# One attention and feed-forward kernel: where the output weights' sums are made, which banks the queries behind a burst use, and which queue carries loads and stores

## The chip, the cores and the metric

The kernel runs on one core of a Trainium2 chip, from one launch. Its time is the device time in microseconds of that core. The kernel before was run 11 times: median 587.55 us, lowest 582.9, highest 592.51. One further execution was recorded by the hardware profiler and took 585.29 us; the recorded span, from its first to its last instruction, is 583.5 us. Every time of day in this text ("at 247.48") is counted in microseconds from the start of that span.

## The reference

All inputs are bfloat16. There are 2048 tokens with 448 features, 16 query heads on 8 key/value heads of width 256, and a feed-forward width of 1792. Attention looks at the last 512 keys of the cache, without a mask.

```python
xn = layernorm(x)                                  # no weights, eps 1e-5
q  = xn @ wq                                       # [2048, 448] @ [448, 16*256]
k, v = k_cache[:, :, -512:], v_cache[:, :, -512:]  # each serves two query heads
p  = softmax(q @ k.T * 256**-0.5)
s  = (p @ v) @ wo                                  # [2048, 16*256] @ [4096, 448]
g  = silu((gelu(xn @ w_gate) * (xn @ w_up)) @ w_down)
out = x + s * g
```

## The kernel before

**Engines and order.** Each engine runs its instructions in the order in which the program emits them. The class `Plan` records every operation with the buffers that it reads and writes, and from these it works out the semaphore waits; nothing is reordered, and there is no cost model. `K.reuse` gives a buffer the readers and writers of whatever held the same memory before it, so that the first write waits for them. DMAs are issued from SP's, ScalarE's (ACT) and Pool's instruction streams. A DMA whose data or whose buffer is not ready holds up everything behind it in the same stream. VectorE is DVE in the code.

**Feed-forward phase (0 to about 115 us).** The layer norm makes xn, tile by tile of 128 tokens. Pool computes the reciprocal standard deviation (`ln_rstd_pool`), VectorE normalises (`ln_norm`), and DMA transposes the tile. The loop over `n` handles two units in a pass, a unit being one block of 128 of the 1792 columns for one chunk of 512 tokens; there are 56 units. TensorE makes gate and up, ScalarE takes gelu (`gu_evac`), VectorE multiplies. Down projections (`down`) stand between passes, for chunks 0 and 1 in this phase and for chunks 2 and 3 beside the first two heads of attention. Their results, the gate values g2, go to memory by SP's queue and are loaded again a tile at a time (`load_g2`, Pool's queue; the profile calls the tile `g` and the memory `g_all`).

In the pass `n == 32` the loads for attention are emitted: Wq and V on Pool's queue, K on SP's queue as DMA transposes, then the output weights wo (`load_wt`) and three tiles of the residual x (`xr`) on Pool's queue.

**Attention.** `m` counts 64 pairs of chunk and head. Queries are made in groups: before the heads `m` = 0, 4, 12, 18, 26, 34, 42, 50 and 58, `q_group` makes two heads at a time, on the four banks of PSUM named AB or the four named BB, in turn. `s_mm(m)` makes the scores of a head in four pieces on AB. ScalarE takes the exponential with its row sum, VectorE the reciprocal and the normalised `pn`, SP issues a DMA transpose of `pn` for every two pieces. `pv(m - 2)` multiplies with V on BB two heads later. The query banks are copied to qT by ScalarE (first bank of a head) and VectorE (second bank).

**Output product.** For chunks 0 to 2 it is a fast product of 2 by 2 blocks with seven block products. `burst(c)` runs it behind the heads 17, 33 and 49. It needs seven operands `wt[:, j]` that are blocks of wo, times 64, and their sums and differences in float16, and sums of the attention outputs (`sr`). The operands are made by `make_wt` on VectorE, three instructions per head in heads 2 to 13, from `wtb`, which lies in the same memory. The 448 output columns are split as 384 + 64; the 384 into two blocks of 192. In the layout before, a block is 128 consecutive columns and 64 further ones, so each block is loaded in two pieces, with rows of 256 and 128 bytes; the second piece waits for the first, as both write the same buffers. The seven products of a burst use B1, B5, B3 and B7, which are the banks BB, and B6 and BN, which are the first two of AB. VectorE and ScalarE add them up (`part`, `fold`) and SP transposes the sums in three DMAs to `sT`. All writes to the source of these transposes wait for the transpose before (one set of buffers, `bx`).

The four tiles of the chunk are finished in the following four heads, by `burst_end` after `pv`; I call them the finishing steps. `wo_end` multiplies with g2, adds the residual in `xr` and stores the tile by SP's queue; `load_next` then loads on Pool's queue the residual of three tiles later into the same slot, which waits for the store, and behind it g2 of two tiles later.

The last chunk is multiplied directly with wo (`wo_mm`, `wo_fin`). Its four loads, on Pool's queue, go into the memory of `wt`, each as soon as the operands below it have been read by the last burst.

Of the kernel before, what the change touches and what calls it, by code (L numbers as in the profile page):

```python
# [5 lines left out]
ACT = mybir.ActivationFunctionType  # L6
ALU = mybir.AluOpType
# [161 lines left out]
def bass_recurrent_scan__sliding_block_cached__geglu_ffn__prompt_kernel(  # L169
# [41 lines left out]
    with es:  # L211
# [62 lines left out]
        NB = 4  # L274
        wt, a_wt, a_w3 = place("wt", [P, 7, Hq, N2], F16)
        wtb, _, _ = place("wtb", [P, 7, Hq, N2], BF16, at=rw)
        b_wt = [[K.buf(rw + (j * Hq + i * Hq // NB) * N2 * 2, Hq // NB * N2 * 2) for i in range(NB)] for j in range(7)]
        w3, _, rw_end = place("w3", [P, NCO, R], F16)
        w3b, _, _ = place("w3b", [P, NCO, R], BF16, at=a_w3)
        b_w3 = [K.buf(a_w3 + i * NCO // NB * R * 2, NCO // NB * R * 2) for i in range(NB)]  # L280
# [68 lines left out]
        def dma(q, o, i, reads=(), writes=()):  # L349
            K.op(q, lambda e, o=o, i=i: e.dma_start(o, i), reads, writes, dma=True)  # L350
# [4 lines left out]
        def act(o, i, func, reads, writes, scale=1.0):  # L355
            K.op("act", lambda e, o=o, i=i: e.activation(o, i, func, scale=scale), reads, writes)  # L356

        def add(eng, o, x, y, reads, writes, op=ALU.add):
            K.op(eng, lambda e: e.tensor_tensor(o, x, y, op), reads, writes)  # L359
# [248 lines left out]
            dma_t(kT[:, g, :, :], A_k_cache[0, g, Sk - W:Sk, :], (), (b_kT[g],))  # L608

        def load_v(g):  # L610
            dma("pool", va[:, g, :, :],
                A_v_cache[0, g, Sk - W:Sk, :].rearrange("(j p) d -> p j d", p=P), (), (b_va[g],))

        def load_wq(g):
            lo, hi = g * HG * Dh, (g + 1) * HG * Dh
            dma("pool", wq[:, :, lo:hi], A_wq[0:K3, lo:hi].rearrange("(k p) f -> p k f", p=P), (), (b_wql[g][0],))
            for e in range(2):
                dma("pool", wqr[R * e:R * e + R, g * HG:(g + 1) * HG, :],
                    A_wq[K3:D, lo:hi].rearrange("p (h e f) -> p h e f", e=2, f=P)[:, :, e, :], (), (b_wql[g][1 + e],))

        wo_view = A_wo.rearrange("(h e p) d -> p e h d", e=2, p=P)
        M1, M2 = slice(0, P), slice(P, N2)

        def load_wt():
            K.reuse([b for x in b_wt for b in x] + b_w3)
            for j, e, n in ((0, 0, 0), (4, 0, 1), (2, 1, 1), (1, 1, 0)):
                dma("pool", wtb[:, j, :, M1], wo_view[:, e, :, n * P:n * P + P], (), b_wt[j])
                dma("pool", wtb[:, j, :, M2], wo_view[:, e, :, 2 * P + n * R:2 * P + n * R + R], (), b_wt[j])
            dma("pool", w3b[:, :, :], A_wo.rearrange("(c p) d -> p c d", p=P)[:, :, D - R:D], (), b_w3)

        def make_wt():
            for i in range(NB):
                hs = slice(i * Hq // NB, (i + 1) * Hq // NB)
                cs = slice(i * NCO // NB, (i + 1) * NCO // NB)
                for o, x, b in [(wt[:, j, hs, :], wtb[:, j, hs, :], b_wt[j][i:i + 1]) for j in (0, 4, 2, 1)] + [
                        (w3[:, cs, :], w3b[:, cs, :], b_w3[i:i + 1])]:
                    yield K.op("dve", lambda e, o=o, x=x: e.tensor_scalar(o, x, WS, None, op0=ALU.mult), b, b)
                for o, x, y in ((6, 2, 4), (4, 4, 0), (5, 2, 4), (3, 1, 5)):
                    yield add("dve", wt[:, o, hs, :], wt[:, x, hs, :], wt[:, y, hs, :],
                              [b_wt[x][i], b_wt[y][i]], b_wt[o][i:i + 1], ALU.subtract)  # L640

        DOWN_AT = {NF + 5: 0, 2 * NF + 1: 1}
        gu_evac(0, 0)
# [5 lines left out]
        for n in range(4, NU, 2):  # L649
            gu_group((n, n + 1), cur)  # L650
            gu_evac(n, cur[0])
            ln_b()
            gu_evac(n + 1, cur[1])
            if ln_t[0] < 8 or n >= 12:
                ln_a()
            cur, nxt = nxt, cur
            if n == 4:
                load_x("sp", 12, 4)
            if n == 8:
                dma("sp", wd[:, :, :], B_w_down.rearrange("(f p) d -> p f d", p=P), (), (b_wd,))  # L660
            if n == 32:
                for g in range(NG):
                    load_wq(g)
                for g in range(Hkv):
                    load_v(g)
                for g in range(Hkv):
                    load_k(g)
                load_wt()
                for t in range(NXR):
                    dma("pool", xr[:, t, :], x_view[:, t, :], (), b_xr[t])  # L670
            if n + 1 in DOWN_AT:
                down(DOWN_AT[n + 1], cur)
                cur, nxt = nxt, cur
# [59 lines left out]
        def wo_end(t, c0, c1, src):  # L733

            s, x, g = t % 2, t % NXR, t % NG2
            hv = [i for i in range(2) if (c0 < CUT, c1 > CUT)[i]]
            bt = [b_tmp[s][i] for i in hv]
            bx = [b_xr[x][i] for i in hv]
            for lo, hi, i, f, reads in src:
                K.op("dve", lambda e, lo=lo, hi=hi, i=i, f=f: e.scalar_tensor_tensor(  # L740
                    out=tmp[:, s, lo:hi], in0=i, scalar=f, in1=g2[:, g, lo:hi],
                    op0=ALU.mult, op1=ALU.mult), list(reads) + [b_g2[g]], bt)
            add("dve", xr[:, x, c0:c1], tmp[:, s, c0:c1], xr[:, x, c0:c1], bt + bx, bx)
            dma("sp", out_view[:, t, c0:c1], xr[:, x, c0:c1], bx, ())

        def load_next(t):
            if t + NXR < NT:
                dma("pool", xr[:, t % NXR, :], x_view[:, t + NXR, :], (), b_xr[t % NXR])
            if t + NG2 < NT:
                load_g2(t + NG2)  # L750

        def load_g2(t):
            dma("pool", g2[:, t % NG2, :], g2d[t], (b_g2d[t],), (b_g2[t % NG2],))

        def wo_fin(c, t4, b, c0=0, c1=D):
            t = c * 4 + t4
            wo_end(t, c0, c1, [(c0, c1, bank[b][:, c0:c1], 0.5, (b_ps[b],))])
            if c1 == D:
                load_next(t)

        o_view = oTh.rearrange("p (h e) (r q) -> p e r h q", e=2, r=2)
        HALF = (slice(0, R), slice(R, P))
# [1 line left out]
        def product(j, b, rhs, hs, first, reads):  # L764

            lst = []

            def pair(lo, hi, l0, r0, l1, r1, st):
                for u, l, r in ((0, l0, r0), (1, l1, r1)):
                    lst.append((bank[b][HALF[u], lo:hi], l, r, st, False))  # L770
            for h in hs:
                pair(0, HC, wt[:, j, h, 0:R], rhs(h), wt[:, j, h, R:P], rhs(h), first and h == hs[0])
            for h in hs[::2]:
                pair(HC, QC, wt[:, j, h, M2], rhs(h), wt[:, j, h + 1, M2], rhs(h + 1), False)
            mms(lst, reads + [b_wt[j][i] for i in sorted({h * NB // Hq for h in hs})], (b_ps[b],))

        def burst(c):
# [70 lines left out]
        def burst_end(c, t4):  # L848
            t = c * 4 + t4
            u = t4 // 2  # L850
            f = 0.5 / (WS * WS)
            wo_end(t, 0, D, [(0, D - R, sT[:, t4, :, :].rearrange("p k n -> p (k n)"), f, b_sT),
                             (D - R, D, sN[:, t4 % 2, u * R:u * R + R], f, (b_sN,))])
            load_next(t)

        LAG = 2
        late = []
# [6 lines left out]
        for m in range(NS):  # L864
            if m in groups:
                for i in range(m, groups[groups.index(m) + 1], 2):
                    q_group(i, (cur, nxt)[i // 2 % 2])
                if m == 0:
                    K.reuse([b for x in b_pT for b in x] + b_pn + b_p32)
            if m > Hq and m % Hq == LAG:  # L870
                K.reuse(b_pn + b_p32)
            s_mm(m)
            if LAG <= m < Hq:
                for x in range(3):
                    next(todo, None)
            if m < LAG:
                down(NQC - LAG + m, nxt)
                if m == LAG - 1:
                    K.reuse(b_oT + [b for y in b_qT[:QS - Q0] for b in y])
                    todo = make_wt()  # L880
                    K.reuse(b_sT + [b_sN])
                    for t in range(NG2):
                        load_g2(t)
            if len(late) == LAG:
                pv(late.pop(0))
            if m > Hq and LAG <= m % Hq < LAG + 4:
                burst_end(m // Hq - 1, m % Hq - LAG)
            if m > Hq and m % Hq == LAG - 1:
                burst(m // Hq - 1)
                if m // Hq == NQC - 1:  # L890
                    K.reuse(b_wo)
                    for i in range(NCO // 8):
                        dma("pool", wo[:, i * 8:(i + 1) * 8, :],
                            A_wo.rearrange("(c p) d -> p c d", p=P)[:, i * 8:(i + 1) * 8, :], (), (b_wo[i],))
            late.append(m)
# [72 lines left out]
```

## Time and profile before

| What | us |
|---|---|
| median of 11 runs | 587.55 |
| profiled execution | 585.29 |
| its span | 583.5 |
| TensorE busy in the span | 554.7 |
| VectorE busy | 376.5 |
| ScalarE busy | 285.8 |
| Pool busy | 52.8 |
| TensorE waits for ScalarE's exponentials | 12.2 |
| TensorE waits for VectorE behind a burst | 8.2 |
| VectorE waits for g2 | 13.3 |

PE is TensorE's multiplication, PEld its loading of weights, DVE is VectorE, ACT ScalarE, POOL Pool; SPq, ACTq and POOLq are the issues of DMAs. A row of the timeline has start, length, engine, line, operation, `out<-in`, and in brackets the idle time before it with what ended it. In a table by stretch, the busy time of each engine (with its instructions) is followed by the granted TensorE clock (1.00 is full speed), the share of time in which the 16 DMA engines were busy, and GB/s. A share can exceed 1, since packets overlap. Waits are inferred: a wait for several things is put down to the one that came last.

### The profile page before, as it was taken

To read this page: it belongs to the slowest core of one execution; us is meant where nothing else is said; L and a number is where in the kernel's file an instruction comes from. 1 tells how busy PE (TensorE), PEld (TensorE's weight loads), DVE (VectorE), ACT (ScalarE), POOL (GpSimd) and SP (SyncE) were. 2 spreads that over 40 slices of the span, in tenths; PEclk is the share of its full clock that TensorE was granted. 3 is DMA by queue.
4 is the path that set the end of the run, shared out by engine and by line. 5 is a ranking of instruction groups with operands and counts; after the bars stand their busy time and mean duration, and the time that the engine had idled before them with its cause. 6 is when DMAs were issued, how large, how long until landed. Compare 5 with 4: busy or idle time off the path is not lost.

```text
span 583.5 us, 11613 instructions
## 1 busy us (share of the span) xinstructions
PE 554.7 (95%) x4444; PEld 288.4 (49%) x4444; DVE 376.5 (65%) x952; ACT 285.8 (49%) x751; POOL 52.8 (9%) x89
## 2 busy tenths in 40 slices
PE   9999999999999899989699998997999989899998
PEld 5554444445443347934244487443445953334455
DVE  6674534443789789549657883687479637876812
ACT  5433333443577485137557830576487115666700
POOL 1120621330000000000200000020000110200001
PEclk9999999999999999999899999998999989989999
DMA  9631599862335557016953830089167362982711
GB/s 290 129 113 42 155 322 157 149 165 76 80 74 127 91 95 124 7 28 114 165 107 72 152 73 19 10 170 174 41 127 156 88 198 44 175 166 49 154 23 56
DMA packets 173479, 66.46 MB, mean 114 GB/s; under 512 B 157872, under 2 KB 169136, under 8 KB 173424
## 3 DMA queue, kind: packets, MB, share of 16 engines
q1 hardware_dynamic: 167552, 48.37, 41.3%
q0 software_dynamic: 5104, 16.78, 11.3%
q8 instruction: 35, 0.57, 0.4%
q10 hardware_dynamic: 768, 0.57, 0.3%
q14 instruction: 20, 0.16, 0.1%
HBM read 23.43 MB, written 3.67 MB: 46 GB/s over the span
## 4 chain that ended last, share of the span: by engine, by line
PE 73%; DVE 14%; DMA 8%; issue 4%; ACT 1%; POOL 0%; DVEq 0%; ACTq 0%
PE bank L365 72%; DVE pn L703 5%; DMA pT<-pn 3%; DMA sT<-xnT 2%; DMA g<-g_all 2%; DVE rden L702 2%; DVE oTh L723 1%; DVE tmp L740 1%; DVE tmp L359 1%; PE bank L482 1%; ACT p L699 1%; DVE xnT L359 1%; DVE wt L359 1%; DVE xr L359 0%; DVE cc L359 0%
## 5 line engine op out<-in xcount | busy, mean ns | idle before, releaser
L699 ACT ACTIVATE p<-bank 128x512 f32<-128x512 f32 x256 | 150.0, 599 | 52.3 <-DVE pn L703 33.8
L703 DVE TENSOR_SCALAR pn<-p,rden 128x512 bf16<-128x512 f32 x256 | 124.6, 487 | 14.7 <-DMA pT<-pn 5.7
L365 PE MATMUL bank<-kT,qT 128*128 128x512 bf16 x512 | 123.1, 381 | 11.2 <-ACT p L699 10.9
L365 PE MATMUL bank<-pT,va 128*128 128x512 bf16 x512 | 125.1, 389 | 2.9 <-DMA pT<-pn 2.6
L365 PE MATMUL bank<-xnT,wq 64*128 64x512 bf16 x768 | 96.5, 380 | 10.7 <-DVE cc L359 8.2
L365 PEld LDWEIGHTS bank<-kT,qT 128*128 128x128 bf16 x512 | 48.8, 98 | 76.5 <-ACT p L699 15.6
L365 PEld LDWEIGHTS bank<-pT,va 128*128 128x128 bf16 x512 | 50.2, 100 | 68.7 <-DMA pT<-pn 8.3
L365 PE MATMUL bank<-xnT,wgu 64*128 64x512 bf16 (+2 forms) x768 | 84.0, 350 | 0.1
L356 ACT ACTIVATE qT<-bank 128x512 bf16<-128x512 f32 x64 | 38.2, 597 | 64.1 <-PE bank L365 62.5
L686 DVE CAST qT<-bank 128x512 bf16<-128x512 f32 x64 | 42.5, 689 | 40.1 <-PE bank L365 40.1
L365 PEld LDWEIGHTS bank<-xnT,wq 64*128 64x128 bf16 x768 | 36.7, 95 | 59.2 <-DVE cc L359 9.0
L531 DVE TENSOR_TENSOR actT<-bank,gl 128x512 bf16<-128x512 f32 x56 | 37.8, 689 | 33.3 <-PE bank L365 26.6
L356 ACT ACTIVATE gl<-bank 128x512 bf16<-128x512 f32 x56 | 33.2, 597 | 49.4 <-PE bank L365 46.2
L365 PEld LDWEIGHTS bank<-xnT,wgu 64*128 64x128 bf16 x768 | 37.1, 94 | 37.0 <-issue 0.7
L699 ACT ACTIVATION_READ_ACCUMULATOR p<-bank 128x1 f32 x256 | 52.9, 207 | 0.0
L702 DVE RECIPROCAL rden<-rsum 128x1 f32<-128x1 f32 x256 | 40.1, 157 | 14.2 <-ACT p L699 14.0
L365 PE MATMUL bank<-wd,actT 128*128 128x448 bf16 x224 | 43.1, 353 | 0.0
L350 POOL DMA_DIRECT2D xr<-in_A_x_dram x16 | 9.0, 564 | 359.8 <-DVE rden L702 204.8
L723 DVE TENSOR_SCALAR oTh<-bank 128x512 f16<-128x512 f32 x48 | 32.8, 684 | 0.1
L365 PEld LDWEIGHTS bank<-wd,actT 128*128 128x128 bf16 x224 | 21.8, 98 | 21.0 <-issue 0.4
L365 PE MATMUL bank<-sr,wt 128*64 128x256 f16 x576 | 31.9, 273 | 0.0
L365 PEld LDWEIGHTS bank<-sr,wt 128*64 128x64 f16 x576 | 31.5, 110 | 0.0
(64 smaller groups left out, 420.8 us busy)
## 6 DMA issues: line engine op xcount, KB each, us to landing
wo<-in_A_wo_dram POOLq DMA_DIRECT2D x4, 896.0 KB, 6.6
wq<-in_A_wq_dram POOLq DMA_DIRECT2D x2, 1536.0 KB, 9.4
va<-in_A_v_cache_dram POOLq DMA_DIRECT2D x8, 256.0 KB, 12.9
wtb<-in_A_wo_dram POOLq DMA_DIRECT2D x4, 512.0 KB, 9.6
pT<-pn SPq DMA_TRANSPOSE x128, 2.8
g_all<-g2w SPq DMA_DIRECT2D x16, 112.0 KB, 1.7
xr<-in_A_x_dram POOLq DMA_DIRECT2D x16, 112.0 KB, 3.4
g<-g_all POOLq DMA_DIRECT2D x16, 112.0 KB, 4.4
```

What stands on the lines that cost most here:

```text
L350: K.op(q, lambda e, o=o, i=i: e.dma_start(o, i), reads, writes, dma=True)
L356: K.op("act", lambda e, o=o, i=i: e.activation(o, i, func, scale=scale), reads, writes)
L359: K.op(eng, lambda e: e.tensor_tensor(o, x, y, op), reads, writes)
L365: ins = e.matmul(o, lhsT=l, rhs=r, start=st, stop=sp, skip_group_check=True)
L482: ins = e.matmul(bank[b][:, 0:w], lhsT=gl[:, 0, 0:P], rhs=gl[:, 0, 0:w], start=True, stop=True)
L531: K.op("dve", lambda e: e.tensor_tensor(actT[:, c % 2, f, :], bank[b + 1], gl[:, s, :], ALU.mult), (b_ps[b + 1], b_gl[s]), (b_actT[c % 2][ ...
L686: K.op("dve", lambda v, s=s, b=b: v.tensor_copy(qT[:, s, 1, :], bank[b + 1]), (b_ps[b + 1],), (b_qT[s][1],))
L699: K.op("act", lambda e, b=b, r=r, z=z: e.activation(p32[:, z, :], bank[b], ACT.Exp, scale=att_scale, accum_out=rsum[:, r:r + 1]), (b_ps[b] ...
L702: K.op("dve", lambda e, r=r: e.reciprocal(rden[:, r:r + 1], rsum[:, r:r + 1]), (b_rsum[r],), (b_rden[r],))
L703: K.op("dve", lambda e, r=r, z=z, y=y, t=t4 % 2: e.tensor_scalar(pn[:, y, t, :], p32[:, z, :], rden[:, r:r + 1], None, op0=ALU.mult), (b_p ...
L723: K.op("dve", lambda v, i=i, b=b, o=o, f=f: v.tensor_scalar(o[:, i, :], bank[b], f, None, op0=ALU.mult), (b_ps[b],), (b_oT[i],))
L740: K.op("dve", lambda e, lo=lo, hi=hi, i=i, f=f: e.scalar_tensor_tensor(out=tmp[:, s, lo:hi], in0=i, scalar=f, in1=g2[:, g, lo:hi], op0=ALU ...
```

## The change

It has five pieces.

- The operands `wt` take other places in the same memory, given by `WAT`: operand 0 lies in place 6, 1 in 3, 2 in 4, 3 in 2, 4 in 5, 5 in 1, 6 in 0. Operands 0 and 4 and the last 64 columns (`w3`) lie outside the memory of x and xn.
- A block of wo is now 192 consecutive columns, loaded in one DMA with rows of 384 bytes. Blocks for operands 0 and 4 and w3 are emitted in the pass `n == 14`, those for 2 and 1 in the pass `n == 30`. The casts with the factor 64 are done by ScalarE (`cast_wt`) from pass 18 on, the subtractions by VectorE (`sum_wt`) from pass 32 on, one in a pass, and from 40 and 44 on two. Operand 6 is computed as 5 minus 0. `make_wt` and its calls in heads 2 to 13 are gone.
- Wq and V are loaded by SP's queue, ahead of K.
- `q_group` begins each set of queries with AB, except for the set before head 12, which begins with BB. Before, the sets at heads 18, 26, 34, 42, 50 and 58 began with BB and that at 12 with AB.
- In `wo_end`, the load of g2 is emitted before the store, the store of all tiles but the last four goes to Pool's queue, and the residual load follows it. A finishing step multiplies with g2 in three instructions instead of two (256, 128 and 64 elements instead of 384 and 64), because of the new order of columns.

```diff
+        WAT = [6, 3, 4, 2, 5, 1, 0]
+        b_wt = [[K.buf(rw + (j * Hq + i * Hq // NB) * N2 * 2, Hq // NB * N2 * 2) for i in range(NB)] for j in WAT]
...
         def load_v(g):
-            dma("pool", va[:, g, :, :],
+            dma("sp", va[:, g, :, :],
...
-            dma("pool", wq[:, :, lo:hi], A_wq[0:K3, lo:hi].rearrange("(k p) f -> p k f", p=P), (), (b_wql[g][0],))
+            dma("sp", wq[:, :, lo:hi], A_wq[0:K3, lo:hi].rearrange("(k p) f -> p k f", p=P), (), (b_wql[g][0],))
...
+        def load_wt(j, e, n):
+            dma("pool", wtb[:, WAT[j], :, :], wo_view[:, e, :, n * N2:(n + 1) * N2], (), b_wt[j])
+
+        def cast_wt(j, i):
...
+            act(o[:, sl, :], x[:, sl, :], ACT.Copy, b[i:i + 1], b[i:i + 1], scale=WS)
+
+        def sum_wt(o, x, y, i):
+            hs = slice(i * Hq // NB, (i + 1) * Hq // NB)
+            add("dve", wt[:, WAT[o], hs, :], wt[:, WAT[x], hs, :], wt[:, WAT[y], hs, :],
+                [b_wt[x][i], b_wt[y][i]], b_wt[o][i:i + 1], ALU.subtract)
+
+        CASTS = [(18, (j, i)) for j in (0, 4, 7) for i in range(NB)] + [(40, (j, i)) for j in (2, 1) for i in range(NB)]
+        SUMS = [(32, (4, 4, 0, i)) for i in range(NB)] + [
+            (44, (o, x, y, i)) for i in range(NB) for o, x, y in ((5, 2, 4), (6, 5, 0), (3, 1, 5))]
...
+            if n == 14:
+                load_wt(0, 0, 0)
+                load_wt(4, 0, 1)
+                dma("pool", w3b[:, :, :], A_wo.rearrange("(c p) d -> p c d", p=P)[:, :, D - R:D], (), b_w3)
+            if n == 30:
+                K.reuse([b for j in (1, 2, 3, 5, 6) for b in b_wt[j]])
+                load_wt(2, 1, 1)
+                load_wt(1, 1, 0)
+            for i in range(2 if n >= 40 else 1):
+                if CASTS and n >= CASTS[0][0]:
+                    cast_wt(*CASTS.pop(0)[1])
+            for i in range(2 if n >= 44 else 1):
+                if SUMS and n >= SUMS[0][0]:
+                    sum_wt(*SUMS.pop(0)[1])
...
-            dma("sp", out_view[:, t, c0:c1], xr[:, x, c0:c1], bx, ())
-
-        def load_next(t):
-            if t + NXR < NT:
-                dma("pool", xr[:, t % NXR, :], x_view[:, t + NXR, :], (), b_xr[t % NXR])
-            if t + NG2 < NT:
+            if t + NG2 < NT and c1 == D:
                 load_g2(t + NG2)
+            dma("sp" if t >= NT - 4 else "pool", out_view[:, t, c0:c1], xr[:, x, c0:c1], bx, ())
+            if t + NXR < NT and c1 == D:
+                dma("pool", xr[:, x, :], x_view[:, t + NXR, :], (), b_xr[x])
...
-            wo_end(t, 0, D, [(0, D - R, sT[:, t4, :, :].rearrange("p k n -> p (k n)"), f, b_sT),
-                             (D - R, D, sN[:, t4 % 2, u * R:u * R + R], f, (b_sN,))])
-            load_next(t)
+            two = lambda x, lo, hi: x[:, 0:2 * N2].rearrange("p (n d) -> p n d", n=2)[:, :, lo:hi]
+            wo_end(t, 0, D, [(lambda x: two(x, 0, P), sT[:, t4, 0:2, :], f, b_sT[:2]),
+                             (lambda x: two(x, P, N2), sT[:, t4, 2, :].rearrange("p (n d) -> p n d", n=2), f, b_sT[2:]),
+                             (lambda x: x[:, 2 * N2:D], sN[:, t4 % 2, u * R:u * R + R], f, (b_sN,))])
...
-                    q_group(i, (cur, nxt)[i // 2 % 2])
+                    q_group(i, (cur, nxt)[((i - m) // 2 + (m == Q0 + QS)) % 2])
...
-            if LAG <= m < Hq:
-                for x in range(3):
-                    next(todo, None)
```

## The prediction

> **What bounds the kernel now.** I read the page first. TensorE is busy for 554.7 of 583.5 us, so 28.8 us is all that a better order can return, unless a stall also slows the clock. Then the table of waits, to see what TensorE waited for, and who waited for the rest:
>
> ```profile
> PE 554.7 (95%) x4444; PEld 288.4 (49%) x4444; DVE 376.5 (65%) x952; ACT 285.8 (49%) x751; POOL 52.8 (9%) x89
> ...
> PE bank L365 <- ACT p L699: 12.2, 7, 4.0
> DVE tmp L740 <- DMA g<-g_all: 13.3, 4, 5.0
> PE bank L365 <- DVE cc L359: 8.2, 3, 2.7
> ```
>
> The columns of a wait are total us, times, longest. Busy time by stretch puts them in place (stretch, length, PE, PEld, DVE, ACT, POOL, granted clock, DMA share, GB/s):
>
> ```profile
> 110.00:148.00 38.00, 38.00 (x239) 18.43 (x236) 16.49 (x39) 17.71 (x43) 7.99 (x9) 1.00 0.46 116
> 170.00:196.00 26.00, 23.37 (x110) 9.67 (x107) 24.93 (x78) 18.09 (x57) 0.00 (x0) 1.00 0.65 119
> 243.00:252.00 9.00, 6.27 (x102) 5.06 (x98) 4.25 (x9) 1.24 (x3) 0.00 (x0) 1.00 0.14 29
> 280.00:300.00 20.00, 15.63 (x73) 6.16 (x72) 13.30 (x40) 10.53 (x32) 2.14 (x4) 0.91 0.85 153
> 467.00:484.00 17.00, 13.09 (x146) 7.73 (x144) 7.10 (x16) 3.63 (x7) 1.76 (x2) 0.90 0.53 166
> ```
>
> The feed-forward phase has no gap. The gaps are where VectorE makes the weights' sums (170 to 196, VectorE 24.93 of 26), right behind each burst (243, 360, 471), and in the four finishing steps behind a burst (280 to 300, and their like at 394 and 509). The timeline shows that last stall whole:
>
> ```profile
> 278.17 0.54 POOL L350 DMA_DIRECT2D xr<-in_A_x_dram  x1 [6.45 <-DVE rden L702]
> 278.70 0.62 POOL L350 DMA_DIRECT2D g<-g_all  x1
> ...
> 283.97 0.56 DVE L740 SCALAR_TENSOR_TENSOR tmp<-sT,g 128x384 f32<-128x384 bf16 x1 [3.58 <-DMA g<-g_all]
> ...
> 286.69 1.03 PE L365 MATMUL bank<-kT,qT 128*128 128x512 bf16 x2 [4.04 <-ACT p L699]
> 287.51 3.20 PE L365 MATMUL bank<-pT,va 128*128 128x512 bf16 x8
> ```
>
> Pool's queue holds the residual load xr until the SP store of the same slot has landed, the gate load g2 stands behind it, VectorE waits 3.58 us for g2, the exponentials wait for VectorE, TensorE waits 4.04 us and then runs at half clock: its eight matmuls take 3.20 us where others take 1.89.
>
> **Part 1, sums of the weights.** VectorE loses 16 casts of 353 ns, 4 of 287 and 16 subtractions of 555 (15.7 us) in heads 2 to 13. There its starts of a head's first normalisation lie 4.18 us apart (165.59 to 194.86 over 7 heads), against 3.45 us of TensorE (two blocks of eight in 1.73 each). Without them VectorE needs about 3.0. The stalls they cause are 1.00, 0.15, 0.28 and, for the query group of head 12, 1.32: **-2.75 us**. In the feed-forward phase the same work is hidden: a pass of two units is 3.02 us of a full TensorE; ScalarE has 1.25 us in it and gets one or two casts of 768 elements, 0.81 us each (from its 597 ns for 512 and 381 for 256), at most 2.87; VectorE has 1.34 and gets at most two subtractions, 2.45. Uncovered they would cost 15.4 and 8.9 us. The first cast waits in ScalarE's order for its data, and ahead of VectorE's work for tile 10 Pool has three more issues (1.15 + 1.15 + 1.68 = 4.0 us from 35.8, so that a normalisation at 38.9 waits 1.8 us). Both delays fall into the ten microseconds of the first down projection (40 to 51), which needs neither: 0.
>
> **Part 2, loads moved.** Wq and V (14 issues, some 0.6 us each by SP's row for w_down) go from Pool's queue to SP's, ahead of the K transposes and behind the gate stores that end at 76.5. 5.5 MB at the 350 GB/s seen at 76 to 84 is 16 us, so the first K lands near 100; its scores start at 120.8. The weight loads lose the second piece and the wait between pieces (13.6 us at most) and go to 36 to 50 and 65 to 78, where DMA is at 0.15 to 0.5. They are needed at 52 and 94: 0.
>
> **Part 3, score banks first.** The burst's products end at 247.48; the first query group now starts at 250.21, on banks that VectorE frees last. On the score banks it starts at 247.5; the second starts at 250.5, when those banks are free (250.15). The third, at 253.5, needs VectorE's copies of the first, which stand behind the four folds, which wait for the transpose sT: the first copy ends at 254.55, as before. So 1.1 of 2.73 us comes back one group later; the third group starts at 254.6 for 256.25: **-1.65 us, twice**. The later groups, and heads 26, 42 and 58, I put at 0 (their score banks are emptied while the value product runs; at the other end a 0.25 us gap goes or comes).
>
> **The third burst is different.** There sT needs 7.07 us, not 2.4, beside the loads of wo, so VectorE's copies start at 482.7 and the third group at 483.4, whatever the order of the banks. The new places of the weights in memory delay wo: its first quarter overlaps operands that are read to 467 (issued at 458.8 now), the other three the one read last, 471.6. So three loads instead of two leave from 471.9 on. The two hold the DMA engines to 480.3 and sT lands at 481.0. One more is 0.92 MB at about 320 GB/s, 2.9 us: third group at 486.3 for 483.4. TensorE then has stood from 477.6 on and comes back at half clock; the same drop cost 1.53 us at 474 (16 matmuls in 3.26 for 1.73), but there behind the wait. Together **+4.4 us**. Here the Trainium skill speaks for less: *DMA: Bandwidth & Descriptors*, Queues, rings and completion order, has an engine take turns between queues packet by packet. By that sT would need at most twice 2.4 us whatever stands in the other queue, the third load would add nothing, and the sum would be 1.5. The row, where it landed only 0.7 us after the loads ended, decides for 4.4; 1.5 stays as the low end, 6 as the high one (sT of the step before is slowed too).
>
> **Part 4, order of Pool's queue.** The g2 load now stands ahead of store and residual load. Counted from the first finishing step of a burst: store issued at 1.5, landed by 6.5 (SP's take 1.7 us; for a store on Pool, which no row shows, I take 5, near the 5.6 of its slowest residual load; the low end is 1.7), residual load issued to 7.0, then the critical g2, landed 5.3 later at 12.3. Its reader comes at 13.2. So VectorE's waits of 3.58, 3.01 and 1.70 go. The half-clock stretches behind them go too: 0.42 + 1.31, 1.32 + 0.41, and 1.59. On this *TensorE: Matmul & The Clock Gate*, Why this matters for your kernels, warns of gaps over some 3 us; here gaps of 4.04 and 3.29 dropped the clock, and so did one of 2.13, while two of 2.73 did not. By the page the third stretch would have to be left in (1.6 us less gained); the row takes it out. Against it, each finishing step has one more instruction: 384 elements (551 ns) become 256 and 128, which the 64-element row (218) makes 418 + 285, so +0.15, four times 0.6. Sum: -(3.58 + 1.73 - 0.6) - (3.01 + 1.73 - 0.6) - (1.70 + 1.59 - 0.6) = **-11.5 us**. VectorE needs 4.4 us for a head in these steps against TensorE's 3.45, so small gaps remain. Stores leave SP's queue, which gives the transposes 0.34 us each: 0.
>
> **Sum.** -2.75 - 3.3 + 4.4 - 11.5 = -13.15 on the profiled execution's 585.29 gives 572.1. That execution lies 2.26 under the median of the runs, 587.55, so I forecast **574.4 us**.
>
> **Rivals.** (a) The third load of wo adds nothing[...]: 571.5. For it: fair turns; against: the 7.07 us. (b) The g2 wait comes back by the new way, store to residual load to g2 in one queue. From a store of over 6 us on, each further microsecond is VectorE's and then TensorE's, and the clock drops again. DMA shares of 1.0 to 1.3 in this stage speak for it, the 0.9 us of room above against. Half of part 4 lost: 580; all of it, which is the change not doing what it says: 586 to 588, the same as before. (c) Slower: one SP queue carries Wq, V and K in order, and the first scores wait for K. From 120.8 on each microsecond late is one lost, with 1.5 for the clock; it ends above the time before when K lands after 132.5, 56 us behind the first issue where the rates above give some 24: 590. K's transposes took up to 13.7 us each with other loads beside them, which speaks for it; but only the first is awaited.
>
> **How the numbers follow.** Likeliest 0.50 at 574.4 (571 to 578 by its own terms), (a) 0.18, half of (b) 0.20, all of (b) 0.06, (c) 0.06. The low end takes in (a) with smaller leftovers, the high one half of (b): 570 to 581. About 0.3%, 1.8 us, is what a measurement can tell from no change: faster 0.88, same 0.05, slower 0.07.
>
> **What would show it.** Right: no gap from 163 to 200; query matmuls straight behind the products of the first two bursts, with a gap near 1.1 us before the third group; a long gap, 6 us or more, there in the last burst; no wait of tmp for g2, full clock in the finishing steps. Wrong: TensorE gaps before 120, gelu behind a cast, K arriving after 120, or Pool's residual load still between VectorE and g2.

## The result, and the profile after

The changed kernel takes 580.34 us (median of 12 runs, 576.93 to 582.73), the kernel before 586.77 (47 runs). The ratio is **0.99, with a 95% interval of 0.9873 to 0.9927**: some 6 us less, where 13.15 less was forecast. The profiled execution took 580.54 us, its span is 578.7.

The head of the page of the changed kernel:

```profile
PE 550.0 (95%) x4444; PEld 288.6 (50%) x4444; DVE 372.2 (64%) x944; ACT 298.0 (51%) x771; POOL 45.0 (8%) x83
```

Its table of waits, columns as before:

```profile
POOL xr L351 <- DMA out_dram<-xr: 40.3, 13, 4.7
...
PE bank L366 <- DVE qT L701: 13.4, 3, 8.9
...
PE bank L366 <- DMA pT<-pn: 8.8, 6, 2.2
...
PE bank L366 <- ACT p L714: 1.4, 3, 0.6
```

VectorE's wait for g2 (13.3 us before) is gone, and TensorE's waits for the exponentials fell from 12.2 to 1.4 us. In their place stand 13.4 us for VectorE's query copies (1.2 before), three waits, one behind each burst, and 8.8 for the transposes of pn (2.6 before). The same stretches as before, and one more, 356 to 366 (length, PE, PEld, DVE, ACT, POOL, granted clock, DMA share, GB/s):

```profile
110.00:148.00 38.00, 38.00 (x238) 18.39 (x233) 18.92 (x45) 17.93 (x43) 0.00 (x0) 1.00 0.20 53
170.00:196.00 26.00, 24.95 (x132) 11.02 (x132) 19.89 (x60) 18.93 (x59) 0.00 (x0) 1.00 0.71 142
243.00:252.00 9.00, 7.88 (x88) 4.10 (x84) 3.92 (x11) 3.40 (x7) 0.00 (x0) 1.00 0.16 31
280.00:300.00 20.00, 18.58 (x131) 8.11 (x131) 12.92 (x34) 11.70 (x31) 0.79 (x2) 1.00 0.61 128
356.00:366.00 10.00, 7.22 (x56) 2.83 (x52) 4.76 (x10) 2.24 (x5) 0.00 (x0) 0.83 0.12 24
467.00:484.00 17.00, 8.05 (x52) 3.00 (x50) 4.68 (x9) 2.01 (x4) 0.00 (x0) 0.70 0.51 157
```

VectorE's load in heads 2 to 13 fell from 24.93 to 19.89 of 26 us. Behind the last burst TensorE stands for more than half of 17 us. The timeline shows both kinds of gap:

```profile
244.66 0.82 PE L366 MATMUL bank<-xnT,wq 64*128 64x512 bf16 x6
...
250.22 1.62 DVE L360 TENSOR_TENSOR xnT<-cc 64x256 bf16<-64x256 f32 x4 [2.80 <-DMA sT<-xnT]
251.76 2.47 DVE L701 CAST qT<-bank 128x512 bf16<-128x512 f32 x4
252.50 0.82 PE L366 MATMUL bank<-xnT,wq 64*128 64x512 bf16 x6 [1.62 <-DVE qT L701]
...
264.16 0.54 POOL L351 DMA_DIRECT2D g<-g_all  x1 [194.57 <-DVE tmp L755]
264.82 0.55 POOL L351 DMA_DIRECT2D out_dram<-xr  x1
267.19 0.54 POOL L351 DMA_DIRECT2D xr<-in_A_x_dram  x1 [1.83 <-DMA out_dram<-xr]
...
273.06 1.90 PE L366 MATMUL bank<-pT,va 128*128 128x512 bf16 x8 [2.15 <-DMA pT<-pn]
...
478.24 1.46 PE L366 MATMUL bank<-xnT,wq 64*128 64x512 bf16 x6 [8.95 <-DVE qT L701]
```

The queries start at 244.66, with no idle time ahead of them. The four copies of the first two groups (251.76) stand in VectorE's queue behind the four folds (250.22), and these wait for a transpose. So the third group waits 1.62 us, and 8.95 in the last burst. In the finishing steps Pool issues g2, then the store, then the residual load; VectorE no longer waits for g2, but the transposes of pn now land late.

To see what each step was worth, I cut the spans at events that every profile has. The **query stage** runs from VectorE's first addition behind a burst to the first score matmul of the next head; eight **heads** follow, to the first query matmul of the next group. Without a gap and at full clock the query stage is 16.24 us (it occurs so in a run below) and the eight heads are 27.6 (16 blocks of 1.73). The changed kernel was profiled three times; the second row is the execution shown above, the third the mean of all three.

| | to the first burst | query stage 1, 2, 3 | heads 1, 2, 3 | rest | span |
|---|---|---|---|---|---|
| before | 243.59 | 18.92, 18.92, 21.97 | 35.55, 33.88, 33.15 | 177.5 | 583.5 |
| changed | 240.84 | 17.81, 20.43, 27.79 | 31.65, 32.40, 30.91 | 176.9 | 578.7 |
| changed, mean of three | 240.48 | 18.03, 20.00, 27.28 | 31.52, 31.23, 31.41 | 176.9 | 576.8 |
| forecast | 240.84 | 17.27, 17.27, 26.37 | 30.84, 29.74, 30.46 | 177.5 | 570.35 |

Against the mean of three the forecast misses 6.5 us: 3.5 in the first two query stages, 0.9 in the third, 3.1 in the heads; the other columns give back about 1.

### The profile page after: what moved, and what is told of

It is laid out like the page before. It is cut to its first block, busy times and chain, and to the rows that moved or that the text cites. A ratio compares the mean times of both kernels' runs of the same rounds, so it can differ in the third digit from the quotient of the medians.

```text
span 578.7 us, 11601 instructions
## 1 busy us (share of the span) xinstructions
PE 550.0 (95%) x4444; PEld 288.6 (50%) x4444; DVE 372.2 (64%) x944; ACT 298.0 (51%) x771; POOL 45.0 (8%) x83
## 4 chain that ended last, share of the span: by engine, by line
PE 78%; DMA 9%; DVE 9%; issue 2%; ACT 1%; DVEq 0%; ACTq 0%
PE bank L366 77%; DMA pT<-pn 5%; DMA sT<-xnT 4%; DVE pn L718 3%; DVE xnT L360 1%; DVE tmp L360 1%; DVE tmp L755 1%; DVE rden L717 1%; DVE oTh L738 1%; PE bank L483 1%; DVE xr L360 0%; ACT p L714 0%; ACT qT L357 0%; DVE oT L738 0%; DVE qT L701 0%
## 5 line engine op out<-in xcount | busy, mean ns | idle before, releaser
L366 PE MATMUL bank<-pT,va 128*128 128x512 bf16 x512 | 120.9, 379 | 8.8 <-DMA pT<-pn 8.8
L366 PE MATMUL bank<-kT,qT 128*128 128x512 bf16 x512 | 121.6, 379 | 1.5 <-ACT p L714 1.4
L366 PE MATMUL bank<-xnT,wq 64*128 64x512 bf16 x768 | 99.1, 387 | 14.4 <-DVE qT L701 13.4
L717 DVE RECIPROCAL rden<-rsum 128x1 f32<-128x1 f32 x256 | 40.3, 157 | 16.6 <-ACT p L714 16.5
L351 POOL DMA_DIRECT2D g<-g_all x16 | 8.7, 542 | 365.8 <-DVE tmp L755 365.7
```

The lines of the kernel that those rows point to most:

```text
L366: ins = e.matmul(o, lhsT=l, rhs=r, start=st, stop=sp, skip_group_check=True)
L717: K.op("dve", lambda e, r=r: e.reciprocal(rden[:, r:r + 1], rsum[:, r:r + 1]), (b_rsum[r],), (b_rden[r],))
```

## The experiments

Ratios are to the kernel before in runs on the same chip, with their 95% intervals. The kernel before had a median of 584.15 us beside the first four experiments, 585.93 beside the next four and 583.63 beside the last four.

**1. Stores back on SP's queue.** Changed kernel, one line:

```diff
-            dma("sp" if t >= NT - 4 else "pool", out_view[:, t, c0:c1], xr[:, x, c0:c1], bx, ())
+            dma("sp", out_view[:, t, c0:c1], xr[:, x, c0:c1], bx, ())
```

> The changed kernel with one thing undone: all stores of finished tiles go to SP's queue again; the g2 load stays ahead of the residual load on Pool's queue. Theory A, the stores on Pool's queue travel beside the transposes of p and make them late (3.5 to 6.0 us to landing in the finishing steps, where 2.8 is usual), so that TensorE now waits for pT instead of g2: the waits of TensorE for pT in the finishing steps (8.8 us in all) fall to about half, 4 us, and the time to some 576. Theory B, the lateness comes from the amount of traffic in these steps, whichever queue has the store: waits for pT stay at 7 to 9 us and the time within 1 us of the changed kernel, 580.3. Theory C, the store on SP delays the transposes behind it more: 582 or more.

578.27 us, ratio 0.9893 [0.9824, 0.9962], against 0.99 of the changed kernel. TensorE's waits for pT fell from 8.8 to 5.8 us, and the heads take 31.76, 30.32 and 30.92 us. This lies between theories A and B: fewer waits, but a ratio like that of the changed kernel. Which queue carries the stores makes no difference that can be measured.

**2. The loads of wo out of the last burst.** Changed kernel; the four loads are emitted one per head at `m` = 54 to 57:

```diff
-                if m // Hq == NQC - 1:
+            if NS - 10 <= m < NS - 10 + NCO // 8:
+                i = m - (NS - 10)
+                if i == 0:
                     K.reuse(b_wo)
-                    for i in range(NCO // 8):
-                        dma("pool", wo[:, i * 8:(i + 1) * 8, :],
+                dma("pool", wo[:, i * 8:(i + 1) * 8, :],
```

> The changed kernel with the four loads of wo emitted in heads 54 to 57, behind the finishing steps of the last burst, in place of inside the burst. Theory A, these loads alone make the transpose sT of the last burst late (10.4 us to landing, 2.4 without): the gap of 8.95 us before the third query group falls to about 1.6, the half-clock stretch behind it goes, and the time falls by 8 to 9 us to some 572. Theory B, part of the gap comes from the burst's own order: the gap stays at 4 us or more and the gain is 5 us or less. Theory C, the loads cost the same again by slowing the transposes of p in heads 54 to 58: the time stays within 2 us of 580.3.

584.45 us, ratio 1.0023 [0.9962, 1.0084]: slower than the changed kernel, by more than theory C allowed. The timeline:

```profile
466.93 0.82 PE L366 MATMUL bank<-xnT,wq 64*128 64x512 bf16 x6 [2.62 <-DVE qT L701]
...
514.06 3.60 PE L366 MATMUL bank<-pT,va 128*128 128x512 bf16 x8 [9.97 <-DMA pT<-pn]
```

The gap behind the last burst shrinks from 8.95 to 2.62 us (the query stage from 27.79 to 20.72), so the loads were its cause. But they hold up a transpose of pn instead, and the eight heads take 42.60. The traffic by queue from 503 to 514 (packets, MB, share of the engines):

```profile
q0 software_dynamic: 597, 2.48, 82.8%
q1 hardware_dynamic: 1125, 0.28, 16.0%
```

A transpose that usually lands after 2.7 to 2.8 us took 17.5 here, beside 2.48 MB on Pool's queue (q0). The loads hold up whatever transpose is under way.

**3. The old order of banks.** Changed kernel:

```diff
-                    q_group(i, (cur, nxt)[((i - m) // 2 + (m == Q0 + QS)) % 2])
+                    q_group(i, (cur, nxt)[i // 2 % 2])
```

> The changed kernel with the old order of banks for all query groups. Theory A, the new order only moves the gap behind a burst from the first to the third group: 2.73 us before the first group of each burst comes back, the gaps of 1.62, 2.78 and 8.95 before the third go (the last to about 3, since sT is late there too), and the time is equal or up to 2 us lower, 578 to 580.5. Theory B, the new order is worth its forecast 3.3 us on the first two bursts: 582 to 584.

581.76 us, ratio 0.9975 [0.9932, 1.0017], close to theory B. Timeline:

```profile
246.47 0.82 PE L366 MATMUL bank<-xnT,wq 64*128 64x512 bf16 x6 [2.76 <-DVE cc L360]
...
479.21 1.46 PE L366 MATMUL bank<-xnT,wq 64*128 64x512 bf16 x6 [5.76 <-DVE qT L701]
```

The gap ahead of the first group is back. In the last burst 2.73 + 5.76 = 8.49 us stand for 8.95: there (2.73 ahead of the first group, 5.76 ahead of the third) the order of banks is worth next to nothing, as forecast, since the third group waits for sT with either. (In the second profile of this kernel, experiment 11, the third query stage is 26.07 us, 1.2 less than the mean of the changed kernel.)

**4. Finishing steps without their loads.** Changed kernel. The loads of g2 and of the residual are left out except for the last tiles, so most tiles are finished with other tiles' values:

```diff
-            if t + NG2 < NT and c1 == D:
+            if t + NG2 < NT and c1 == D and t >= NT - 5:
                 load_g2(t + NG2)
...
-            if t + NXR < NT and c1 == D:
+            if t + NXR < NT and c1 == D and t >= NT - 5:
```

> The changed kernel without the loads of residual and g2 in the finishing steps of the three bursts, except for the last one; tiles of these chunks are finished with values of other tiles, and only the stores are left on Pool's queue. Theory A (traffic beside the transposes makes pT late): the waits of TensorE for pT in the finishing steps, 8.8 us in all, fall to 2 us or less, and the time by 5 to 7 us to some 574. Theory B (VectorE's pace of 4.30 us for a head against TensorE's 3.45 sets the gaps, and the late pT only shows where they fall): TensorE's idle time in the four finishing heads stays within 1 us of before, and the time at 579 or more.

576.02 us, ratio 0.9854 [0.9782, 0.9927]. The heads take 30.75, 29.79 and 30.72 us, mean 30.4, where 27.6 would be TensorE's own. The timeline says why:

```profile
275.08 0.60 PE L366 MATMUL bank<-kT,qT 128*128 128x512 bf16 x2 [0.58 <-ACT p L714]
277.01 1.90 PE L366 MATMUL bank<-pT,va 128*128 128x512 bf16 x8 [1.33 <-DMA pT<-pn]
```

The result lies between the two theories. Without these loads the heads still take 2.8 us per burst more than 27.6. TensorE stands behind scores that VectorE normalised late (2.9 us in the table of waits) and for transposes of pn (3.9, of 8.8 before), of which one pair per burst lands after 4.1 to 5.3 us even here. How the 2.8 us divide between VectorE's pace and these transposes was not separated. The loads add 1.0 us per burst (31.4 in the changed kernel); that is read from the profiles, as the intervals of the two ratios overlap.

**5. The changed kernel again**, with no edit.

> The changed kernel itself, for a comparison on the same chip with the three kernels beside it. Theory A, what a single profile shows behind a burst and in the finishing steps is the rule: the gaps before the third query group are again near 1.6, 2.8 and 9 us. Theory B, part of them is chance of one execution: the gap of the second burst or the half clock behind it is gone, and the stretch from the second burst to the third is 2 us or more shorter than the 110.9 us of the first profile.

579.7 us, ratio 0.9904 [0.9852, 0.9957]; query stages 18.13, 20.74, 27.08 and heads 30.62, 30.20, 32.60. The gaps before the third group are 1.72, 2.72 and 8.37 us, as theory A had it.

**6. Folds behind the queries.** Changed kernel. `burst` returns the four folds and the third transpose as a function, which is called behind the query groups of the next head:

```diff
-            for r, n, slot in ((0, 0, 2), (1, 1, 3), (0, 1, 0), (1, 0, 1)):
-                fold(r, n, slot)
-            dma_t(sT[:, :, 2, :], xs[2], bx, (b_sT[2],))
             K.reuse([b for y in b_qT for b in y])
+            def folds():
+                for r, n, slot in ((0, 0, 2), (1, 1, 3), (0, 1, 0), (1, 0, 1)):
+                    fold(r, n, slot)
+                dma_t(sT[:, :, 2, :], xs[2], bx, (b_sT[2],))
+            return folds
...
             if m > Hq and m % Hq == LAG:
+                folds()
                 K.reuse(b_pn + b_p32)
...
-                burst(m // Hq - 1)
+                folds = burst(m // Hq - 1)
```

> The changed kernel with the four folds and the transpose behind them emitted behind the query groups that follow a burst, so that VectorE's copies of the queries no longer stand behind them. Theory A, the third query group waits for these copies only because of that order: the gaps of 1.6, 2.8 and 8.95 us vanish with the half-clock stretches behind them (1.4 and 2.6 us), some 17 us, and of this 1.6 us per burst comes back as VectorE does the folds just where it is the slower engine; time 566 to 570. Theory B, the transposes of the burst hold the copies up in another way, or the later folds and sT now stop the finishing steps: the time falls by less than 5 us, to 575 or more.

**565.19 us, ratio 0.9688 [0.961, 0.9766]**: the best version here, 14.5 us under the changed kernel of the same four experiments, and just under theory A's 566 to 570. Its busy times by stretch:

```profile
243.00:252.00 9.00, 9.00 (x101) 4.77 (x98) 4.60 (x9) 3.39 (x7) 0.00 (x0) 1.00 0.17 31
280.00:300.00 20.00, 19.95 (x145) 8.76 (x145) 12.76 (x34) 11.70 (x31) 0.54 (x1) 1.00 0.55 110
467.00:484.00 17.00, 16.11 (x91) 6.82 (x88) 14.69 (x43) 11.74 (x34) 2.75 (x5) 1.00 0.59 156
```

and the timeline behind the first burst:

```profile
247.25 1.28 DVE L701 CAST qT<-bank 128x512 bf16<-128x512 f32 x2
...
257.48 1.61 DVE L360 TENSOR_TENSOR xnT<-cc 64x256 bf16<-64x256 f32 x4
```

The copies come at 247.25, 4.5 us earlier than in the changed kernel, the folds at 257.48, when the queries are done. All three query stages take 16.24 us, with the clock at 1.00. In the last burst sT still takes 10.0 us, but nobody waits for it. The heads grow to 31.95, 33.14 and 35.26: 6.2 us of the 16.6 saved in the query stages go back there.

**7. As 6, with Pool adding the residual.**

```diff
+            if t >= NT - 4:
+                add("dve", xr[:, x, c0:c1], tmp[:, s, c0:c1], xr[:, x, c0:c1], bt + bx, bx)
             if t + NG2 < NT and c1 == D:
                 load_g2(t + NG2)
+            if t < NT - 4:
+                add("pool", xr[:, x, c0:c1], tmp[:, s, c0:c1], xr[:, x, c0:c1], bt + bx, bx)
```

> The kernel with the folds behind the query groups, and the addition of the residual in the finishing steps done by Pool instead of VectorE (0.62 us of VectorE's 4.30 us for a head there). Theory A, VectorE's pace sets most of TensorE's idle time in the finishing steps: 4 steps by 0.62 us less for each of three bursts, 7 us at most and 4 to 6 us as gaps, below the kernel without that. Theory B, the late transposes set it: the same time within 1.5 us. Theory C, Pool's addition is slow, or shares something with VectorE, and holds store and loads up in Pool's queue: slower.

567.19 us, ratio 0.9724 [0.9634, 0.9814]: no gain over 6. The intervals overlap, so the times alone do not tell theory B from theory C; the timeline shows C's mechanism:

```profile
263.69 1.49 DVE L718 TENSOR_SCALAR pn<-p,rden 128x512 bf16<-128x512 f32 x1
263.84 1.05 POOL L360 TENSOR_TENSOR xr<-tmp,xr 128x448 bf16<-128x448 f32 x1
...
265.29 0.48 DVE L718 TENSOR_SCALAR pn<-p,rden 128x512 bf16<-128x512 f32 x1
```

VectorE is spared an addition of 0.62 us, but the normalisation beside Pool's addition takes 1.49 instead of 0.48: it ends 0.29 us after Pool.

**8. The weights' sums back in heads 2 to 13.** Changed kernel; the casts go to VectorE and the calls from the feed-forward passes to the heads, three to a head:

```diff
+            if LAG <= m < Hq:
+                for x in range(3):
+                    if CASTS:
+                        cast_wt(*CASTS.pop(0)[1])
+                    elif SUMS:
+                        sum_wt(*SUMS.pop(0)[1])
```

> The changed kernel with the casts and subtractions for the weights done by VectorE in heads 2 to 13 again, three in a head; the loads stay early and in one piece. Theory A, the first part of the change is worth the waits that it removes, 2.75 us by forecast and 1.7 by the one profile: 1.7 to 3 us slower than the changed kernel, all before 196 us. Theory B, it is worth nothing, as the slower start is caught up by the first burst: within 1 us.

585.91 us, ratio 1.0 [0.9953, 1.0048], 6.2 us more than the changed kernel beside it and more than theory A's 1.7 to 3. The first burst comes at 247.68 us for 240.07. Timeline at head 12:

```profile
192.91 0.82 PE L366 MATMUL bank<-xnT,wq 64*128 64x512 bf16 x6 [0.86 <-DVE oTh L733]
...
197.41 1.46 PE L366 MATMUL bank<-xnT,wq 64*128 64x512 bf16 x6 [3.46 <-DVE oTh L733]
```

In the new order the queries of head 12 begin on BB, which wait for VectorE's copy of the attention output (oTh). With VectorE behind, that wait is 3.46 us and the clock drops. So this is more than Part 1 undone: the sums and the order of banks at head 12 belong together.

**9. Only the order of g2.** Kernel before:

```diff
             add("dve", xr[:, x, c0:c1], tmp[:, s, c0:c1], xr[:, x, c0:c1], bt + bx, bx)
+            if t + NG2 < NT and c1 == D:
+                load_g2(t + NG2)
             dma("sp", out_view[:, t, c0:c1], xr[:, x, c0:c1], bx, ())
...
-            if t + NG2 < NT:
-                load_g2(t + NG2)
```

> The kernel before with the fourth part's order alone: the load of g2 ahead of the store and of the residual load; stores stay on SP's queue and the finishing step keeps its two multiplications. Theory A, VectorE's pace sets a floor of 30 to 31 us for the eight heads behind a burst's queries (34.2 on average in the kernel before, 31.5 in the changed one, 30.4 in the run without reloads, 27.6 if TensorE never waited): 3 to 4 us for each burst, 9 to 11 in all, 575 to 578. Theory B, the forecast's working, with only one small gap left: 13.3 us (11.5 and the 1.8 of the added instructions), 572 to 573. Theory C, the gain of the changed kernel needs Pool's stores too: less than 5 us.

579.33 us, ratio 0.993 [0.9895, 0.9966]: 4.3 us by the medians, theory C's size, though not for its reason: in experiment 1 the changed kernel did without Pool's stores. No wait for g2 is left, but:

```profile
288.81 2.93 PE L365 MATMUL bank<-pT,va 128*128 128x512 bf16 x8 [3.09 <-DMA pT<-pn]
```

Where VectorE waited for g2, TensorE now waits for a transpose. The heads take 34.28, 29.97 and 32.51, together 5.8 us less than before.

**10. As 6, with the old order of banks** (the edit of 3).

> The kernel with the folds behind the query groups, with the old order of banks. Theory A, the two belong together: with the folds out of the way the new order of banks is worth the whole gap of 2.73 us before the first group of each burst, 8.2 us, so this kernel takes 573 to 574. Theory B, the late folds are what pays and the order of banks is of little weight: 567 or less.

577.38 us, ratio 0.9872 [0.9823, 0.992]. Timeline:

```profile
246.31 0.82 PE L366 MATMUL bank<-xnT,wq 64*128 64x512 bf16 x6 [2.77 <-DVE cc L360]
```

The query stages are 20.65, 20.60 and 20.62, each 4.4 us over 16.24: the gap of 2.7 and 1.6 to 1.7 of half clock. With the folds late, the order of banks is worth 12.2 us by the medians (577.38 - 565.19, beside medians of the kernel before that differ by 2.3) and 10.8 by the ratios. Folds late alone give 3.8 over experiment 11, the order alone 3.1 (below), both together some 16. Theory A's 573 to 574 is missed by 3.4 us, as half clock stands behind each gap; in kind it holds.

**11 and 12. The order of banks with the folds in their place**: the kernel of 3, and the changed kernel, side by side once more.

> The changed kernel with the old order of banks once more, beside the changed kernel on the same chip. Theory A, by the profiles the stretches from burst to first scores are 19.2, 20.8 and 27.2 us here and 18.1, 20.7 and 27.1 in the changed kernel, so the order of banks is worth some 1 to 2 us, with what head 12 gives. Theory B, the difference of the two earlier comparisons with the kernel before (0.9975 and 0.990) is real: 4 us. Theory C, nothing.

> The changed kernel again, for the comparison with the old order of banks on one chip: 1 to 2 us below it by theory A, 4 by theory B, the same by theory C. Its stretch from the second burst's first addition to the first scores is 20.5 us or more if the half clock behind that gap is the rule, and 19 if it was chance in two profiles.

581.19 us, ratio 0.9967 [0.9933, 1.0001], and 578.1, ratio 0.9894 [0.9855, 0.9933]. The new order is worth 3.1 us by the medians, between theories A and B. In this third profile of the changed kernel the second query stage is 18.83 us: its gap of 2.65 us left the clock alone. So the half clock behind that gap, there in the two profiles before, is not the rule.

## Why the prediction was wrong

The change works by the mechanisms forecast, but gives half of the time. In the profiles the miss of 6.5 us lies mostly in two terms, the first two query stages of Part 3 (3.5) and the heads of Part 4 (3.1). The runs put it on Part 4: the order of banks alone is worth 3.1 us (experiments 11 and 12) where I had 3.3, the order of g2 alone 4.3 (experiment 9) where my working gave 13.3. By the steps:

**Part 1 was right in its sum, partly by luck.** The first burst comes 2.75 us earlier in the first profile, as summed, and 3.1 on average. But a wait at head 12, which I had put all gone, is left: 1.05, 0.21 and 0.67 us in the three profiles. So the waits gave less than summed, and some 1.0 us in each profile came from elsewhere, which I had not forecast; from where was not settled. Experiment 8 shows that the step carries more in the changed kernel than I gave it: it keeps the new order of banks at head 12 affordable.

**Part 2 was right.** TensorE has no gap from 110 to 148; the first transposed K came near 100. ScalarE waited 3.4 us for the first weights and VectorE 2.0 for Pool, both under the down projection that was named as cover. Two readings in the forecast were off without effect: in the kernel before the scores start at 120.2 and not 120.8, and from 65 to 78 the DMA share is 0.91 and not up to 0.5 (Wq and V, which the change moves away).

**Part 3: right in kind, mis-sized in the profile.** "1.1 of 2.73 us comes back one group later" was 1.62 in the first burst and 2.78 in the second, since the awaited transpose landed after 3.0 and 4.2 us and not after 2.4. Behind the second the clock fell to 0.83 in its stretch, 1.5 us more, which I had not priced. So the first two query stages gave +0.2 us on average and not -3.3. The kernel before had been profiled with both its gaps of 2.73 at full clock; of the other profiles with the old order, seven of eight such stages lose 1.4 to 1.9 us of half clock there (query stages of 20.4 to 20.8). By runs (11 against 12) the order is worth 3.1, close to the 3.3. The interval of either ratio is wider than that agreement.

**The third burst: right.** Forecast was a gap of 8.7 us (477.6 to 486.3); it was 8.95, with three loads leaving together at 463.44. The term +4.4 measured +5.3, since the half clock behind it cost 2.6 us and not 1.53. Rival (a), that the third load adds nothing, did not occur: sT took 10.4 us. I had taken from the turns between queues in *DMA: Bandwidth & Descriptors*, Queues, rings and completion order, that sT needs at most twice 2.4 us. The DMA view of the changed kernel has, by queue (packets, MB, share), from 465 to 470 and then from 472 to 474:

```profile
q0 software_dynamic: 354, 1.50, 91.5%
q1 hardware_dynamic: 19, 0.00, 0.4%
...
sT<-xnT SPq DMA_TRANSPOSE x1, 10.4
...
q0 software_dynamic: 157, 0.66, 88.7%
q1 hardware_dynamic: 157, 0.04, 8.9%
```

The transpose, on q1, moves nothing until 469.25, 3.7 us after its issue (1.2 us for one with no load beside it). Then the queues do take turns, 157 packets each, but a packet of the loads has some 4 KB and one of the transpose 256 bytes. So the page's turns by packet agree with this part of the trace; "at most twice" was my own step and does not follow from them. What held the first packet back is open. Experiment 2 gives the other side: without the loads sT takes 4.0 us.

**Part 4 is the step that failed**: the sum of -11.5, which takes VectorE's waits for g2 off TensorE's time one for one and puts the effect on the transposes at 0. The single forecasts in it held: g2 is never waited for, VectorE's starts in these steps lie 4.3 us apart (4.4 forecast), a store on Pool lets the residual load go 2.4 to 4.8 us after its issue (5 taken), and the half clock in these heads shrank by 5.2 us (5.05 forecast). But TensorE's idle time there shrank by 3.2 us and not by 6.5. In the mean of three profiles its waits for exponentials in these heads went from 9.5 to 1.5 us, and those for transposes of pn rose from 2.6 to 7.5. So the 24 heads gave 8.4 us in the profiles and not 11.5.

The transposes had been late before the change too. First the wait in the kernel before, then the transposes of pn issued from 264 to 284 (number, median us to landing) in the kernel before, the changed kernel and experiment 4:

```profile
PE bank L365 <- DMA pT<-pn: 2.6, 6, 0.8
...
pT<-pn SPq DMA_TRANSPOSE x8, 4.3
...
pT<-pn SPq DMA_TRANSPOSE x10, 4.1
...
pT<-pn SPq DMA_TRANSPOSE x10, 2.8
```

In the kernel before, this lateness lay under the wait for g2: one transpose issued at 279.81 took 6.1 us and landed at 285.95, just ahead of the end of TensorE's 4.04 us wait at 286.69. With that wait gone, TensorE stands for the transposes. Without the loads they land after 2.8 us, and the 24 heads take 91.3 us in sum, where the forecast had 91.0 and the changed kernel has 94.2 (93.4 to 95.0 in its three profiles). So 2.9 of the 3.1 us missing in the heads go with the loads. VectorE's pace is not what the sum missed: four steps at 4.3 us against 3.45 of TensorE are up to 3.4 us per burst, of which I charged only the extra multiplication (0.6), but the rest was in the time before and stayed there. Before, the 24 heads took 19.8 us more than 3 times 27.6. Less 11.5, that leaves 8.3, which is what they take with no loads at all (8.5); with them 11.4 are left.

Rival (b) had the number, 580, by another road, so by chance: it needed VectorE to wait for g2 again. Rival (c) did not occur.

**Where the gain went.** Experiments 6 and 10 settle it for the bursts. The new order of banks takes the gap from ahead of the first group, and VectorE's queue gives it back ahead of the third, because query copies that are ready stand behind folds that wait for a DMA. With that moved, the order is worth some 12 us, and the slow sT of the last burst costs nothing.

**What stays open.** Experiment 9 (heads 96.8 us in sum) and the changed kernel (94.2) do the same with g2, and experiment 1 excludes the queue of the stores; from where the 2.6 us between them come was not settled. Why sT takes 3.0 to 4.2 us in the changed order was not tested. Loads of wo spread thinly over the last heads were not tried.

## What to carry to other kernels

Before pricing the removal of a wait, look in the trace for what ends just behind it in that stage: transfers that already land late under its cover (here 4.3 us where 2.8 is usual) become the next wait, and that part is not saved. When reordering takes away one wait, look in the in-order queue of the engine that must answer next for an instruction that waits for a DMA, and move ready work ahead of it; here that was worth more than twice the change itself. A bulk load moved away from one latency-bound transfer should be placed where no other is in flight.

## What the runs showed of the hardware

**Half clock after short gaps.** Of the gaps of 1.18 to 2.01 us among the queries behind bursts (8) none dropped the clock. Of those of 2.39 to 2.78 us (23 in all profiles) 15 did: the next 16 matmuls took 2.1 to 3.3 us instead of 1.73. Gaps of 3.85 and more always did. In the kernel before, the gap of 2.73 left the clock alone twice and dropped it once. In the heads shorter gaps dropped it as well: 7 of 16 of those of 1.64 to 2.25 us (16 matmuls in 5.15 us or more instead of 3.46), with a gap of 0.5 to 0.7 in the 6 us before 5 of the 7, but also before 4 of the other 9. *TensorE: Matmul & The Clock Gate*, What's actually happening, has a free-running window of some 3.4 us, which fits that chance decides, but not that so many gaps below 3 us drop the clock.

**Transposes with small traffic beside them.** The second transpose of a burst took 3.0 to 3.4 us behind the first and 3.8 to 4.2 behind the second in all nine profiles with the new order, against 2.4 before. Each had one packet of an instruction queue in its interval. So had three slow ones with the old order (2.9 to 3.4 us), and none of the 63 others behind the first two bursts of the 14 profiles (2.4 to 2.5 us); the DMA view of the changed kernel, 354 to 358:

```profile
q8 instruction: 1, 0.02, 1.8%
...
sT<-xnT SPq DMA_TRANSPOSE x1, 4.2
```

That is a correlation only.

**Pool's addition holds VectorE up.** In experiment 7 the normalisation or multiplication that VectorE ran beside Pool's addition of 1.05 us ended 0.29 us after it, all 12 times. The normalisations among them (10) took 0.80 to 1.90 us, against 0.48 to 0.49 alone. *GPSIMD Engine Reference*, 8. Key points, says that the two share their ways into SBUF; here the time lost, 0.3 to 1.4 us and 1.0 on average, was more than the 0.62 moved.
